# Table cosines by a quarter turn, LayerNorm statistics moved to ScalarE, and a later long-lag tail in an S4 block with a gated MLP

## The chip, the cores and the metric

The kernel runs on one core of a Trainium2 chip. A time is the device time of one execution in microseconds (us), quoted as the median of several executions. Where two kernels are compared, the ratio is the mean time of one kernel's fast runs over that of the other's fast runs of the same rounds, so it is not quite the ratio of the medians. A "span" is the profiled execution alone and is about 2 us shorter than the timed figure.

Five engines work side by side: PE (TensorE, matrix products), DVE (VectorE), ACT (ScalarE), POOL (GpSimd) and SP (which issues the transfers). Each has its own instruction list, and waits tie the lists together. A scheduler orders each list from the program text, so editing one part can reorder others.

## The reference, cut to what matters

```python
h  = x + S4(layernorm(x))               # x is [1, 2048, 640]
h2 = h + MLP(layernorm(h))
# S4: a convolution of length 2048 per channel, with
P = exp(dt*A * l)                       # complex, l = 0..2047, 128 states, 640 channels
K = einsum("dn,dnl,dn->dl", C, P, dt*B).real
y = irfft(rfft(u, 4096) * rfft(K, 4096))[:2048] + u * Dskip
# MLP
out = (sigmoid(x @ w_gate) * (x @ w_up)) @ w_down      # F = 1728
```

The powers `P` are complex exponentials, so building them needs a sine and a cosine of large phases. The kernel builds them from two tables, A and B, in four chunks of 160 channels. It multiplies the tables on PE to get the convolution kernel, and does the convolution with Fourier matrices on PE over four sequence blocks.

## The kernel before

The cosine needed two steps on ScalarE: an absolute value of the phase, in place, and a Sin with a bias from a [128,1] tile of pi/2.

```python
def cos_of(out, ph, scale):
    nc.scalar.activation(ph, ph, AF.Abs)
    act_fn(out, ph, AF.Sin, scale=-scale, bias=hpi[:, 0:1])

def trig_a(c):                                   # sines and cosines of table A, chunk c
    ...
    for k0, n in ((0, 6), (6, 5), (11, 5)):
        ph = tabp.tile([P, 6, W], F32, name="a_ph", tag="ph", bufs=2)
        for k in range(n):
            nc.vector.tensor_scalar(ph[:, k], phi[:, o:o + W], ..., MAGIC16, ALU.mult, ALU.add)
        p16 = ...                                # the low 16 bits of ph, as int16
        act_fn(f(sn), p16, AF.Sin, scale=SIN_SCALE16)
        cos_of(f(cs), p16, SIN_SCALE16)
```

The phase is an fp32 number to which a large constant was added, so its low 16 bits hold the phase modulo one turn. `table_a(c)` multiplies exponentials with these sines and cosines on VectorE; its tile `tabA` has one buffer that every chunk uses in turn. `kmm(c)` multiplies table A by table B on PE into `pk`, ScalarE evicts `pk` to `kts`, and from it come `kv` and `klast`. `forward(b)` is the Fourier transform of sequence block b, with ScalarE evicting `ps_z` to `zs`.

```python
def ln_stats(st, mv, src, r):                    # one row of LN statistics on VectorE
    for hh in range(2):
        nc.vector.bn_stats(st[:, r, hh, :], src(r)[:, 320 * hh:320 * hh + 320])
    nc.vector.bn_aggr(mv[:, r, :], ...)

def ln_stats_act(src, mv, rr, junk):             # the same on ScalarE, two passes a row
    for i, r in enumerate(rr):
        nc.scalar.activation(junk(i), src(i), AF.Identity, accum_out=acc[:, 0, r:r + 1])
    ...
    for i, r in enumerate(rr):
        nc.scalar.activation(junk(i), src(i), AF.Square, bias=acc[:, 0, r:r + 1], accum_out=acc[:, 1, r:r + 1])

    # main order, cut
    for r in range(8):
        ln_stats(st, mv, ur, r)                  # blocks 1 and 2 on VectorE
    ln_stats_act(..., range(8, 16), ...)         # blocks 3 and 4 on ScalarE
    trig_a(0); chain_b(0); norm(0); table_a(0); ...; forward(0); kvs = [kmm(0)]
    trig_a(1); norm(1); chain_b(1); norm(2); norm(3)
    for b in range(1, NB):
        ... forward(b)
    for c in range(NC - 1):
        ...                                      # kmm(c), inverse of c-1, chain_b(c+1)
        Vt = kspec(c, ...)                       # spectra of the kernel, products, long-lag spectra
        table_a(c + 1, ...); trig_b(c + 2); ...; trig_a(c + 2)
    kvs.append(kmm(NC - 1)); ...
    Vl = kspec(NC - 1, ...)                      # its long-lag spectra before the last inverse
    inv0(NC - 1, Vl, ...)
    mlp(...)
```

## Time and profile before

| | before |
|---|---|
| median of 3 runs | 391.68 us (391.44 to 392.13) |
| profiled span | 389.7 us |
| the MLP alone, first Sigmoid (182.4) to the end | 207.3 us |
| second chunk's `kv` complete | 131.9 us |
| the four tables A complete | 54.7, 82.0, 114.0, 156.4 us |

First the profile page of the kernel before: busy time per engine, then the busy share in 40 equal slices of 9.7 us, in tenths. PEclk is PE's granted clock, in tenths of full speed.

```profile
PE 317.8 (82%) x2466; PEld 197.3 (51%) x2466; DVE 290.6 (75%) x659; ACT 266.7 (68%) x481; POOL 13.5 (3%) x16
...
PE   1533378881569899948999999997999999999996
...
DVE  2999998979799869499999899999999222112131
ACT  6988979969969877655556675556765558755500
...
PEclk9976589997769999996999999998999999999999
```

From the 19th slice on, PE is nearly full: that is the MLP. Ahead of it (0 to 180 us) VectorE and ScalarE are the fuller ones in most slices up to the 13th. So a gain has to come from there.

Next the busy time of each engine in three stretches of before. The columns are the stretch, its length, then busy us with instruction counts for PE, PEld, DVE, ACT and POOL, then the granted clock, the DMA share and GB/s.

```profile
96.00:112.00 16.00, 6.79 (x51) 4.47 (x51) 14.04 (x32) 15.99 (x23) 0.00 (x0) 0.71 0.06 22
134.00:157.00 23.00, 21.34 (x357) 19.18 (x355) 18.52 (x42) 18.08 (x35) 0.00 (x0) 1.00 0.28 73
180.00:380.00 200.00, 196.87 (x1118) 104.25 (x1117) 137.35 (x269) 117.90 (x220) 3.70 (x3) 0.99 0.16 56
```

From 96 to 112 ScalarE is busy every moment and PE works 6.8 of 16 us. The timeline of that stretch (start, duration, engine, line, operation) shows why, and what follows from it 35 us later:

```profile
102.76 0.68 ACT L390 CAST zs<-ps_z 128x640 bf16<-128x640 f32 x1
103.33 0.97 ACT L224 ACTIVATE a_cs<-a_ph,hpi 128x800 bf16<-128x800 int16 x1
104.19 0.87 ACT L224 ACTIVATE a_sn<-a_ph 128x800 bf16<-128x800 int16 x1
...
105.34 1.12 ACT L246 ACTIVATE a_ph<-a_ph 128x800 int16<-128x800 int16 x1
...
110.09 0.72 ACT L390 CAST zs<-ps_z 128x640 bf16<-128x640 f32 x1
110.86 3.36 PE L389 MATMUL ps_z<-u,c_G 128*128 128x320 bf16 x12 [4.81 <-ACT zs L390]
...
143.79 0.83 DVE L288 TENSOR_TENSOR tabA<-tabEA,tabE 128x1280 bf16<-128x1280 bf16 x1 [3.49 <-PE pk L409]
```

Two evictions of `ps_z` lie 7.3 us apart, with Sin, Abs, Sin and others between them. PE waits 4.81 us for the second. PE then does what is left of the second chunk (its `kv`) and the third chunk's products late, and VectorE waits 3.49 us for the latter before it may overwrite the table's buffer.

The costliest table-A groups on ScalarE (busy us, mean ns), and one kind of LN pass:

```profile
L246 ACT ACTIVATE a_ph<-a_ph 128x800 int16<-128x800 int16 x8 | 8.9, 1108 | 0.0
L224 ACT ACTIVATE a_cs<-a_ph,hpi 128x800 bf16<-128x800 int16 x8 | 7.8, 970 | 0.0
L224 ACT ACTIVATE a_sn<-a_ph 128x800 bf16<-128x800 int16 x8 | 6.9, 868 | 0.0
L361 ACT ACTIVATE ln_junk<-u,ln_acc 128x640 bf16<-128x640 bf16 x8 | 6.5, 818 | 0.0
L246 ACT ACTIVATE a_ph<-a_ph 128x960 int16<-128x960 int16 x4 | 5.2, 1290 | 0.0
```

### The profile page before, as it was taken

The numbers are of one execution on the slowest core, as the hardware profiler recorded it, in microseconds if no ns is written. First come the engines' busy times: TensorE is split into PE (matmuls) and PEld (weight loads), VectorE is DVE, ScalarE is ACT, GpSimd is POOL, SyncE is SP. The second block draws the span as 40 slices with busy tenths as digits, with TensorE's granted clock in tenths as the row PEclk, the third lists the DMA queues.
The fourth block names the chain that finished last, engine by engine and source line by source line (L and its number), as shares of the span: only waits on it lengthen the run. The fifth ranks groups of instructions, "written<-read, shape, count | busy, mean of one in ns | idle before, by whom it ended". The sixth has DMA issues, their size and how long they took to land.

```text
span 389.7 us, 6462 instructions
## 1 busy us (share of the span) xinstructions
PE 317.8 (82%) x2466; PEld 197.3 (51%) x2466; DVE 290.6 (75%) x659; ACT 266.7 (68%) x481; POOL 13.5 (3%) x16
## 2 busy tenths in 40 slices
PE   1533378881569899948999999997999999999996
PEld 0522156560337788834444664443664445744463
DVE  2999998979799869499999899999999222112131
ACT  6988979969969877655556675556765558755500
POOL 0030200020000000010000100000100000000000
PEclk9976589997769999996999999998999999999999
DMA  7940000431011532699960003000003000010001
GB/s 174 395 199 1 2 0 2 143 149 67 35 67 41 133 103 67 212 276 349 363 238 0 2 2 135 0 3 1 0 17 119 2 0 2 0 69 1 0 19 50
DMA packets 28496, 33.49 MB, mean 86 GB/s; under 512 B 16305, under 2 KB 23858, under 8 KB 28210
## 3 DMA queue, kind: packets, MB, share of 16 engines
q1 hardware_dynamic: 28466, 33.08, 25.5%
q8 instruction: 19, 0.31, 0.3%
q14 instruction: 11, 0.09, 0.1%
HBM read 23.88 MB, written 9.18 MB: 85 GB/s over the span
## 4 chain that ended last, share of the span: by engine, by line
PE 40%; DVE 34%; ACT 17%; DMA 4%; issue 2%; POOL 2%; SPq 1%; DVEq 0%; ACTq 0%; POOLq 0%
PE ml_po L760 11%; PE ml_pu L730 8%; PE ml_pg L730 7%; DVE u L621 5%; DVE u L620 4%; DVE u L624 3%; DVE u L623 3%; ACT zs L390 2%; ACT a_ph L246 2%; ACT a_cs L224 2%; PE ps_xk L461 2%; DVE ml_hm L741 2%; PE ps_z L389 2%; PE pk L409 2%; ACT xk L463 2%
## 5 line engine op out<-in xcount | busy, mean ns | idle before, releaser
L389 PE MATMUL ps_z<-u,c_G 128*128 128x320 bf16 x256 | 46.5, 338 | 29.2 <-ACT Z L390 12.9
L730 PE MATMUL ml_pg<-lnT,Wg 128*128 128x512 bf16 x260 | 66.5, 381 | 0.0
L730 PE MATMUL ml_pu<-lnT,Wu 128*128 128x512 bf16 x260 | 65.7, 383 | 0.0
L760 PE MATMUL ml_po<-Wd,ml_hm 128*128 128x320 bf16 x416 | 61.1, 304 | 0.0
L760 PEld LDWEIGHTS <-ml_hm 128*128 128x128 bf16 x416 | 40.7, 99 | 18.5 <-issue 1.5
L389 PEld LDWEIGHTS <-c_G 128*128 128x128 bf16 x256 | 27.1, 109 | 44.4 <-issue 31.9
L738 ACT ACTIVATE ml_sg<-ml_pg 128x512 bf16<-128x512 f32 x52 | 31.0, 596 | 25.7 <-PE ml_pg L730 19.5
L741 DVE TENSOR_TENSOR ml_hm<-ml_ub,ml_sg 128x512 bf16<-128x512 bf16 x52 | 21.8, 420 | 34.4 <-ACT ml_ub L740 34.4
L740 ACT CAST ml_ub<-ml_pu 128x512 bf16<-128x512 f32 x52 | 30.4, 584 | 22.5 <-PE ml_pu L730 22.4
L730 PEld LDWEIGHTS <-Wu 128*128 128x128 bf16 x260 | 25.6, 99 | 30.8 <-issue 0.5
L730 PEld LDWEIGHTS <-Wg 128*128 128x128 bf16 x260 | 25.6, 99 | 28.1 <-issue 0.6
L620 DVE TENSOR_TENSOR u<-Z,S 128x1280 bf16<-128x1280 bf16 x36 | 29.3, 815 | 0.0
L621 DVE TENSOR_TENSOR u<-Z,S 128x1280 bf16<-128x1280 bf16 x36 | 29.3, 816 | 0.0
L409 PE MATMUL pk<-tabB,tabA 128*128 128x84 bf16 x320 | 17.6, 213 | 12.1 <-ACT kts L410 9.9
L461 PE MATMUL ps_xk<-kv,c_KM 128*128 128x160 bf16 x320 | 24.3, 232 | 2.3 <-ACT xk L463 1.0
L461 PEld LDWEIGHTS <-c_KM 128*128 128x128 bf16 x320 | 22.6, 98 | 3.8 <-issue 3.2
L409 PEld LDWEIGHTS <-tabA 128*128 128x128 bf16 x320 | 15.7, 105 | 15.4 <-issue 11.4
L636 PE MATMUL ps_y<-VR,c_IV 128*128 128x320 bf16 x96 | 19.7, 300 | 2.3 <-ACT ml_ub L740 2.3
L390 ACT CAST zs<-ps_z 128x640 bf16<-128x640 f32 x24 | 15.8, 688 | 7.1 <-DMA dz<-zs 3.8
L624 DVE TENSOR_TENSOR u<-u,u 128x1280 bf16<-128x1280 bf16 x24 | 19.6, 816 | 0.0
L623 DVE TENSOR_TENSOR u<-u,u 128x1280 bf16<-128x1280 bf16 x24 | 19.6, 815 | 0.0
L702 ACT ACTIVATE ln<-h,ln_nmr,ln_rstd 128x640 bf16<-128x640 bf16 x14 | 11.8, 910 | 7.8 <-DVE ln_nmr L369 7.8
(133 smaller groups left out, 518.8 us busy)
## 6 DMA issues: line engine op xcount, KB each, us to landing
dz<-zs SPq DMA_DIRECT2D x12, 320.0 KB, 2.2
Z<-dz SPq DMA_DIRECT2D x6, 640.0 KB, 6.6
u<-in_A_u_dram SPq DMA_DIRECT2D x4, 640.0 KB, 5.8
c_KM<-s4c_KM SPq DMA_DIRECT2D x1, 2560.0 KB, 12.6
h<-in_A_u_dram SPq DMA_DIRECT2D x4, 640.0 KB, 3.8
dxk<-xk SPq DMA_DIRECT2D x16, 160.0 KB, 2.4
S<-dxk SPq DMA_DIRECT2D x4, 640.0 KB, 11.2
Wg<-in_B_w_gate_dram SPq DMA_DIRECT2D x4, 520.0 KB, 6.8
```

What stands on the lines that cost most here:

```text
L389: MM(ps[:, ri, 0:UH], lhsT=G[:, ft, hf, ri, r, :], rhs=us[b][:, r, o:o + UH], start=(r == 0), stop=(r == 3))
L409: MM(pk[:, i, :], lhsT=A[:, ri, g].rearrange("p e c -> p (e c)"), rhs=B[:, ri, :, 4 * g:4 * g + 4], start=(ri == 0), stop=(ri == 1))
L461: MM(ps[:, hf, ri * W:ri * W + W], lhsT=KM[:, ft, hf, ri, KI[d] + q, :], rhs=kv[:, j, :], start=(q == 0), stop=(q == len(KD[d]) - 1))
L620: V(t1[:, 0], z, k[:, :, :, o:o + UH], ALU.mult)
L621: V(t2[:, 0], z, k[:, :, ::-1, o:o + UH], ALU.mult)
L623: V(s1[:], s1[:], t1[:], ALU.add)
L624: V(s2[:], s2[:], t2[:], ALU.add)
L730: nc.tensor.matmul(ps[:], lhsT=W[:, dc, f0:f0 + 128], rhs=lnT[:, dc].rearrange("p a b -> p (a b)"), start=(dc == 0), stop=(dc == 4))
L738: nc.scalar.activation(sg[:], pg[:], AF.Sigmoid)
L740: nc.scalar.copy(ub[:], pu[:])
L741: nc.vector.tensor_tensor(hm[:, ft, :], ub[:], sg[:], ALU.mult)
L760: nc.tensor.matmul(po[k][:, c, 0:320], lhsT=hm[:, ft, 128 * lr:128 * lr + 128], rhs=Wd[:, ft, 320 * c:320 * c + 320], start=(start and ft ...
```

## The change

A quarter turn (0.25 in units of a turn) is added to the fp32 phase on VectorE, after the sine has been taken; the cosine is then a plain Sin with no Abs and no bias tile. In addition:

- LN statistics of block 2 (four rows) go from VectorE to ScalarE, so that blocks 2 to 4 are all done there; their small coefficient steps go to GpSimd.
- The norm of a block stands directly before its forward transform, and block 4 comes later, after `corner(0)`; the scheduler's delays of blocks 3 and 4 (`DELAY`) are lowered.
- In the last chunk the long-lag spectra (`later`) follow the inverse, so that their stores no longer stand ahead of the MLP's weight loads.
- A Sigmoid on a dummy element loads that table early.
- The first input load is split, corner terms are merged into one `edge` tile, and PSUM pools are rearranged.

```diff
         for k0, n in ((0, 6), (6, 5), (11, 5)):
             ...
-            act_fn(f(sn), p16, AF.Sin, scale=SIN_SCALE16)
-            cos_of(f(cs), p16, SIN_SCALE16)
+            act_fn(sn[...], p16(ph, n), AF.Sin, scale=SIN_SCALE16)
+            if phs:
+                cosine(*phs.pop())      # add 0.25 on VectorE, then Sin
+            phs.append((k0, n, ph))
+        cosine(*phs.pop())
...
     def norm(b):
-        ln_coef(mv, rstd, nmr, rs)
+        if b:
+            nc.gpsimd.tensor_scalar(rstd[:, rs], mv[:, rs, 1], 1e-5, None, ALU.add)
+            nc.gpsimd.tensor_tensor(rstd[:, rs], rstd[:, rs], mhalf[:, rs], ALU.pow)
+            nc.gpsimd.tensor_tensor(nmr[:, rs], acc[:, 0, rs], rstd[:, rs], ALU.mult)
+        else:
+            ln_coef(mv, rstd, nmr, rs)
...
-    for r in range(8):
+    for r in range(4):
         ln_stats(st, mv, ur, r)
-    ln_stats_act(lambda i: ur(8 + i), mv, range(8, 16), ...)
     trig_a(0)
+    for b in range(1, NB):
+        ln_stats_act(lambda i: ur(4 * b + i), mv, range(4 * b, 4 * b + 4), ...)
...
-    norm(1)
     chain_b(1)
-    norm(2)
-    norm(3)
-    for b in range(1, NB):
-        forward(b)
+    block(1)                            # norm(b), forward(b), with a lower priority
+    block(2)
...
         corner(c)
+        if c == 0:
+            block(3)
...
+    act_fn(hpi[:], hpi[:], AF.Sigmoid)
     kvs.append(kmm(NC - 1))
...
+    # in the MLP part, after the first LN
+    later()                             # the last chunk's long-lag spectra and their stores
```

More of the change, by code (lines that the diff above doesn't have):

```diff
@@ L28 @@
 LATER2 = 300
-DELAY = (0, 0, 300, 600)
+DELAY = (0, 0, 100, 400)
 B_VAL = [0, 4, 2, 6, 1, 5, 3, 7, 256, 260, 258, 262, 512, 516, 768, 772, 1024, 1280, 1536, 1792, 2048]
@@ L33 @@
 NL = 14
-EDGE = [(0, 0), (0, 1), (0, 2), (0, 3)] + [(b, r) for b in range(3) for r in range(2)] + [(b, 0) for b in range(4)]
-SEL = {(0, 3): (10,), (1, 2): (4,), (1, 3): (11, 4, 5), (2, 2): (6,), (2, 3): (12, 6, 7),
-       (3, 0): (0,), (3, 1): (0, 1), (3, 2): (8, 0, 1, 2), (3, 3): (13, 8, 9, 0, 1, 2, 3)}
+EDGE = [(b, 0) for b in range(4)] + [(b, r) for b in range(3) for r in range(2)] + [(0, r) for r in range(4)]
+SEL = {(0, 3): (0,), (1, 2): (4,), (1, 3): (1, 4, 5), (2, 2): (6,), (2, 3): (2, 6, 7),
+       (3, 0): (10,), (3, 1): (10, 11), (3, 2): (8, 10, 11, 12), (3, 3): (3, 8, 9, 10, 11, 12, 13)}
 SELI = {k: i for i, k in enumerate(SEL)}
@@ L81, in host_consts @@
         sel[list(rows), i, 31] = 1.0
+    sel[32, SELI[0, 3], 31] = 1.0
     pick = np.zeros((P, 4, 32))
@@ L91, in host_consts @@
     one = np.zeros((P, 32))
-    one[0, 0] = 1.0
+    one[64, 0] = 1.0
     return {"ident": np.eye(P), "G": G.reshape(P, -1), "KM": KM.reshape(P, -1), "IV": IV.reshape(P, -1), "sel": sel.reshape(P, -1),
@@ L143, in full_kernel @@
     ktp = sc.pool("kts", bufs=2)
-    psk = sc.pool("ps_k", bufs=2, space=PSUM)
+    psk = sc.pool("ps_k", bufs=2, space=PSUM, side="right")
     ps2 = sc.pool("ps_2", bufs=3, space=PSUM)
@@ L159, in full_kernel, with load_u @@
     dl = cp.tile([P, 2, 5], BF16, name="dl")
-    def load_u(b):
-        sy.dma_start(us[b][:], xh[b])
+    def load_u(b, n=4):
+        for r in range(0, 4, n):
+            sy.dma_start(us[b][:, r:r + n], xh[b, :, r:r + n])
     sy.dma_start(dl[:, 0], ins["A_log_dt"].rearrange("(c p) -> p c", p=P))
@@ L169, in full_kernel @@
         if k == 0:
-            load_u(0)
+            load_u(0, 1)
     for b in range(1, NB):
@@ L178, in full_kernel @@
     sel = cload(cp, "sel", [P, len(SEL), 32])
-    dsk = cp.tile([1, D], BF16, name="dsk")
-    sy.dma_start(dsk[:], ins["A_Dskip"].rearrange("(o d) -> o d", o=1))
+    edge = cp.tile([96, D], BF16, name="edge")
+    sy.dma_start(edge[64:65, :], ins["A_Dskip"].rearrange("(o d) -> o d", o=1))
     uh = cp.tile([NL, D], BF16, name="uhead")
@@ L269, in trig_a, with cosine @@
         sn = tabp.tile([P, W // 4, 16, 4], BF16, name="a_sn")
+        phs = []
+        p16 = lambda ph, n: ph[:, 0:n].bitcast(I16).rearrange("p k (g c t) -> p k g c t", c=4, t=2)[:, :, :, :, 0]
+        def cosine(k0, n, ph):
+            nc.vector.tensor_scalar(ph[:, 0:n], ph[:, 0:n], 0.25, None, ALU.add)
+            act_fn(cs[:, :, k0:k0 + n, :].rearrange("p g k c -> p k g c"), p16(ph, n), AF.Sin, scale=SIN_SCALE16)
         for k0, n in ((0, 6), (6, 5), (11, 5)):
@@ L273, in trig_a @@
                 nc.vector.tensor_scalar(ph[:, k], phi[:, o:o + W], 4.0 * (31 - 2 * (k0 + k)) * 2.0 ** -32, MAGIC16, ALU.mult, ALU.add)
-            p16 = ph[:, 0:n].bitcast(I16).rearrange("p k (g c t) -> p k g c t", c=4, t=2)[:, :, :, :, 0]
-            f = lambda t: t[:, :, k0:k0 + n, :].rearrange("p g k c -> p k g c")
-            act_fn(f(sn), p16, AF.Sin, scale=SIN_SCALE16)
-            cos_of(f(cs), p16, SIN_SCALE16)
+            act_fn(sn[:, :, k0:k0 + n, :].rearrange("p g k c -> p k g c"), p16(ph, n), AF.Sin, scale=SIN_SCALE16)
+            if phs:
+                cosine(*phs.pop())
+            phs.append((k0, n, ph))
+        cosine(*phs.pop())
         T["tr", c] = cs, sn
@@ L399, in kmm @@
         kv = ktp.tile([P, 5, W], BF16, name="kv")
-        kr = ktp.tile([NL, W], BF16, name="klast", bufs=1)
         A, B = T["A", c], T["B", c]
@@ L408, in product, with diagonal @@
                     for ri in range(2):
-                        MM(pk[:, i, :], lhsT=A[:, ri, g].rearrange("p e c -> p (e c)"), rhs=B[:, ri, :, 4 * g:4 * g + 4], start=(ri == 0), stop=(ri == 1))
+                        last_mm[0] = MM(pk[:, i, :], lhsT=A[:, ri, g].rearrange("p e c -> p (e c)"), rhs=B[:, ri, :, 4 * g:4 * g + 4], start=(ri == 0), stop=(ri == 1)).ins
                 nc.scalar.copy(kts[:, g0:g0 + GS, :], pk[:])
-        def diagonal(g1, kts):
+        def diagonal(g1, kts, mm):
             ps = ps2.tile([P, 2, 512], F32, name="ps_kv", tag="p2")
@@ L417, in diagonal @@
             dc = slice(o + 4 * g1, o + 4 * g1 + 4 * GC)
-            MM(ps[0:32, 0, 0:4 * GC], lhsT=one[0:1, :], rhs=dsk[0:1, dc], start=True, stop=False, tile_position=(0, 0))
+            with tc.issue_after(mm):
+                MM(ps[0:32, 0, 0:4 * GC], lhsT=one[64:65, :], rhs=edge[64:65, dc], start=True, stop=False, tile_position=(64, 0))
             for c4 in range(4):
@@ L425, in diagonal @@
             for c4 in range(4):
-                for i, q in enumerate((80, 64, 48)):
+                for i, q in enumerate((48, 64, 80)):
                     MM(pl[:, :, c4], lhsT=last[:, i, c4, :], rhs=kts[:, :, q + c4], start=(i == 0), stop=(i == 2))
             nc.scalar.copy(kv[:, :, 4 * g1:4 * g1 + 4 * GC], ps[:, 0, 0:20 * GC].rearrange("p (j x) -> p j x", j=5))
-            nc.scalar.copy(kr[:, 4 * g1:4 * g1 + 4 * GC], ps[0:NL, 1, 0:4 * GC])
-        prev = None
+            nc.scalar.copy(edge[0:NL, dc], ps[0:NL, 1, 0:4 * GC])
+        prev, last_mm = None, [None]
         for g1 in range(0, G4, GC):
@@ L436, in kmm @@
                 diagonal(*prev)
-            prev = (g1, kts)
+            prev = (g1, kts, last_mm[0])
         diagonal(*prev)
-        return kv, kr
+        return kv
     def fold_back(Vt, t1, t2, fs, w):
@@ L460, in spec @@
                     for q, j in enumerate(KD[d]):
-                        MM(ps[:, hf, ri * W:ri * W + W], lhsT=KM[:, ft, hf, ri, KI[d] + q, :], rhs=kv[:, j, :], start=(q == 0), stop=(q == len(KD[d]) - 1))
+                        mm = MM(ps[:, hf, ri * W:ri * W + W], lhsT=KM[:, ft, hf, ri, KI[d] + q, :], rhs=kv[:, j, :], start=(q == 0), stop=(q == len(KD[d]) - 1)).ins
+            if d == 0:
+                T["mm"] = mm
             dst = S01[:, d, ft, :, :, o:o + W] if d < 2 else xks[:, d - 2, ft]
@@ L480, in kspec, with later @@
             prod((0, 1))
-        for d in range(1, NB):
-            for ft in range(2):
-                spec(d, ft)
-        for d in range(2):
-            for ft in range(2):
-                sy.dma_start(dxk[d, :, ft, :, :, o:o + W], xks[:, d, ft])
-        return Vt
+        def later():
+            for d in range(1, NB):
+                for ft in range(2):
+                    spec(d, ft)
+            for d in range(2):
+                for ft in range(2):
+                    sy.dma_start(dxk[d, :, ft, :, :, o:o + W], xks[:, d, ft])
+        return Vt, later
     def inv0(c, Vt, fs=((0, 1),), done=None):
@@ L495, in inv0 @@
         for a in range(2):
-            MM(pv[:, a], lhsT=ident[:], rhs=hv[:, a], start=True, stop=False)
+            with tc.issue_after(T["mm"]):
+                MM(pv[:, a], lhsT=ident[:], rhs=hv[:, a], start=True, stop=False)
             if a:
-                MM(ps[96:128, a, W:2 * W], lhsT=sel[0:NL, SELI[0, 3], :], rhs=kl[:, o:o + W], start=False, stop=False, tile_position=(0, 96))
+                MM(ps[96:128, a, W:2 * W], lhsT=sel[32:33, SELI[0, 3], :], rhs=edge[32:33, o:o + W], start=False, stop=False, tile_position=(32, 96))
         for fg in fs:
@@ L515, in full_kernel @@
     bases_b(0)
-    for r in range(8):
+    for r in range(4):
         ln_stats(st, mv, ur, r)
-    ln_stats_act(lambda i: ur(8 + i), mv, range(8, 16), lambda i: prp.tile([P, D], BF16, name="ln_junk", tag="y")[:])
     trig_a(0)
+    for b in range(1, NB):
+        ln_stats_act(lambda i: ur(4 * b + i), mv, range(4 * b, 4 * b + 4), lambda i: prp.tile([P, D], BF16, name="ln_junk", tag="y")[:])
     chain_b(0)
@@ L529, in full_kernel, with block @@
     kvs = [kmm(0)]
-    trig_a(1)
-    norm(1)
-    chain_b(1)
-    norm(2)
-    norm(3)
-    for b in range(1, NB):
+    def block(b):
         tc.cur_priority += DELAY[b]
+        norm(b)
         forward(b)
         tc.cur_priority -= DELAY[b]
+    trig_a(1)
+    chain_b(1)
+    block(1)
+    block(2)
     IV = cload(yp, "IV", [P, 4, 2, 2, P], tag="u1")
@@ L548, in full_kernel @@
     h = hs[0]
-    kl = uh
     def corner(c):
         cs = slice(W * c, W * c + W)
-        V(kl[:, cs], kvs[c][1][:], uh[:, cs], ALU.mult)
+        V(edge[32:33, cs], edge[0:1, cs], uh[0:1, cs], ALU.mult)
     for c in range(NC - 1):
@@ L559, in full_kernel @@
         corner(c)
-        Vt = kspec(c, kvs[c][0], prp, yp)
+        if c == 0:
+            block(3)
+        Vt, later = kspec(c, kvs[c], prp, yp)
+        later()
         table_a(c + 1, 2 if c == NC - 2 else 1)
@@ L576, in full_kernel @@
     corner(NC - 1)
-    Vl = kspec(NC - 1, kvs[NC - 1][0], prp, yp)
+    Vl, later = kspec(NC - 1, kvs[NC - 1], prp, yp)
     for r in range(4):
@@ L586, in full_kernel @@
     inv0(NC - 1, Vl, fs=((0,), (1,)), done=done)
-    sc.close("ps_2", "ps_k", "kts")
+    sc.close("ps_k", "kts")
     ZR = [Z0]
@@ L604, in full_kernel, with edges, far @@
     gu = load_gu(nc, wp, ins)
-    load_h(1)
     Wd = load_d(nc, xp, ins)
-    for b in (2, 3):
-        load_z(b)
-        load_s(b)
     VR = {}
+    def edges():
+        V(uh[:], edge[0:NL], uh[:], ALU.mult)
+    def far():
+        later()
+        for b in (2, 3):
+            load_z(b)
+            load_s(b)
     def products(b):
@@ L637, in inverse @@
                     if (b, s) in SELI and not ft:
-                        MM(ps[96:128, 0:UH], lhsT=sel[0:NL, SELI[b, s], :], rhs=kl[:, o:o + UH], start=False, stop=False, tile_position=(0, 96))
+                        MM(ps[96:128, 0:UH], lhsT=sel[0:NL, SELI[b, s], :], rhs=uh[:, o:o + UH], start=False, stop=False, tile_position=(0, 96))
                 hv = hs[b][:, s, o:o + UH]
@@ L643, in inverse @@
                 yield
-    mlp(tc, sc, xp, yp, cp, hs, st2, gu, Wd, ident, oh, ln_coef, ln_stats_act, products, inverse, load_h)
+    mlp(tc, sc, xp, yp, cp, hs, st2, gu, Wd, ident, oh, ln_coef, ln_stats_act, far, edges, products, inverse, load_h)
     sc.close("stream", "weights", "yp", "prod", "xp", "consts", "dram")
@@ L673, in load_d, with mlp @@
     return Wd
-def mlp(tc, sc, xp, yp, cp, hs, st, gu, Wd, ident, oh, ln_coef, ln_stats_act, products, inverse, load_h):
+def mlp(tc, sc, xp, yp, cp, hs, st, gu, Wd, ident, oh, ln_coef, ln_stats_act, later, edges, products, inverse, load_h):
     nc = tc.nc
@@ L680, in mlp @@
     tmp = sc.pool("ml_tmp", bufs=2)
-    psg_p = sc.pool("ml_psg", bufs=2, space=PSUM)
-    psu_p = sc.pool("ml_psu", bufs=2, space=PSUM)
-    pso_p = sc.pool("ml_pso", bufs=2, space=PSUM)
+    psg_p = sc.pool("ml_psg", bufs=2, space=PSUM, side="right")
     mv = big.tile([P, 16, 2], F32, name="ln2_mv")
@@ L691, in prep @@
         r0 = 4 * b
-        ln2 = lns[b] = yp.tile([P, 4, 640], BF16, name="ln2", tag="u0")
+        ln2 = lns[b] = yp.tile([P, 4, 640], BF16, name="ln2", tag="u0" if b else "u3")
         if b:
@@ L718, in mlp @@
     prep(0)
+    tc.cur_priority += LATER
+    later()
+    tc.cur_priority -= LATER
     turn(0)
+    load_h(1)
+    sc.close("ps_2")
+    psu_p = sc.pool("ml_psu", bufs=2, space=PSUM)
+    pso_p = sc.pool("ml_pso", bufs=2, space=PSUM)
     tc.cur_priority += LATER
+    edges()
     products(1)
```

## The prediction

> What bounds it now. One core; the profiled span is 389.7 us, the median 391.68. From about 178.5 us on it is the MLP: by the busy time per stretch, PE is busy 203 of the 210 us from 180 to 390, at a clock near 1, and its longest wait there is 2.3 us. So the MLP takes about 211 us whatever precedes it; a gain must come from the 178 us ahead.
>
> There the bound alternates. From 10 to 54.6 us VectorE is busy 90 to 100% (timeline); the first tabA ends at 54.6 and releases PE. From 63 to 82 and 88 to 140 the chain of waits runs through ScalarE's Sin, Abs, Sin of table A and the zs evictions, while VectorE is 92% busy; it waits about 11 us in all from 82 to 157. From 157 to 178 it is a relay of PE, ScalarE and VectorE for the last chunk.
>
> Removed, added, moved.
> - Twelve Abs on a_ph (8 of 1.108 us, 4 of 1.290) leave ScalarE: about 13 us. The cosines lose their bias tensor: 970 against 868 ns for one shape with and without it, 1.2 us in all. The Trainium skill, "ScalarE: Activation LUTs", "What ACT_TABLE_LOAD costs", gives about 93 ns per pointer operand; the trace shows 102.
> - Twelve fp32 adds come to VectorE. A 640-wide fp32 one in SBUF took 0.475 us; "VectorE: DVE Perf Modes", "The perf-mode tier table", puts it in the 2x mode. Estimate from it: 0.64 and 0.56 us, 7 us in all. VectorE was nearly the bottleneck, so this eats half of the gain.
> - LN statistics of four rows leave VectorE (0.86 us a row, 3.4 us, in the first 22 us) and cost ScalarE 1.53 us a row, 6 us, mostly later; small coefficient steps go to GpSimd.
> - Scheduled order: norms of blocks 2 to 4 follow the first tabA; block 4's forward transform comes later; the first chunk's products precede chain_b of the last.
> - Last chunk: two of four xk evictions with their spectra follow the inverse, and dxk writes no longer block weight loads (queue held from 162 to 170). About 1.2 us.
> - The early Sigmoid load takes 1.28 us off ScalarE at 179.4, but the ml_pg it serves ended later: no gain.
>
> Sum along the new order. First tabA ends near 48 instead of 54.6, but chain_b now ends after it, near 50: kmm starts 4 to 5 us earlier. ScalarE, with the LN rows, reaches the first kts only near 57, so most of this is lost; second tabA ends 1 us earlier (82.0 before), the third about 1.5, with the first products done. From there to the last tabA (156.4) VectorE waits less: 5 to 7 us earlier. MLP starts 6 to 8.5 us earlier; I allow some for new waits.
>
> Predicted 384.5 us, range 380.5 to 389. Faster by over 2%: 0.42; within 2%: 0.57; slower: 0.01.
>
> What would show it: first kmm product at 49 to 51 us; no a_ph Abs; new adds of 0.55 to 0.65 us; ScalarE busy about 9 us less; VectorE about 3 us more, with less idle between 82 and 157; last tabA end 149 to 152; first ml_pu near 171; from there to the end 210 to 212 us.
>
> What would make it wrong: ScalarE's extra LN rows delaying Z, kts and zs evictions more than I sum; zs waiting for its DMA as before (3.0 us at 81); slower adds; VectorE waits in the new order; or, for more gain, the MLP shortening with earlier weights.

## The result, and the profile after

The changed kernel took 385.28 us (385.07 to 385.80, 4 runs) against 391.85 (391.44 to 392.13, 4 runs). The ratio of the fast runs is 0.9835, with a 95% interval of 0.9818 to 0.9852. That is 1.65% faster, within 2%, and 0.8 us above the prediction. The profiled span is 383.1 us.

The page after, and the same stretches:

```profile
PE 315.6 (82%) x2451; PEld 199.7 (52%) x2466; DVE 292.7 (76%) x660; ACT 260.4 (68%) x486; POOL 22.6 (6%) x22
...
PEclk9995667998699789978999999998999999999999
```

```profile
96.00:112.00 16.00, 13.18 (x133) 10.08 (x133) 15.96 (x35) 15.88 (x27) 0.00 (x0) 0.79 0.16 62
134.00:157.00 23.00, 20.52 (x353) 18.05 (x353) 16.91 (x37) 13.44 (x29) 0.00 (x0) 0.94 0.22 56
180.00:380.00 200.00, 195.70 (x1118) 105.00 (x1130) 134.81 (x264) 114.41 (x214) 3.37 (x3) 0.99 0.14 51
```

ScalarE is as full from 96 to 112 as before (15.88 of 16 us), but PE now works 13.2 us instead of 6.8: what the Abs held is spent on evictions. In the timeline they come without the gap, and VectorE waits for PE at the table 0.36 us and not 3.49:

```profile
103.22 0.71 ACT L405 CAST zs<-ps_z 128x640 bf16<-128x640 f32 x1
103.80 0.95 ACT L424 CAST kts<-pk 128x420 bf16<-128x420 f32 x2
104.60 1.33 ACT L405 CAST zs<-ps_z 128x640 bf16<-128x640 f32 x2
...
135.91 0.82 DVE L298 TENSOR_TENSOR tabA<-tabEA,tabE 128x1280 bf16<-128x1280 bf16 x1 [0.36 <-PE pk L423]
```

The groups that answer to those of before (from the lists of ScalarE and of VectorE):

```profile
L371 ACT ACTIVATE ln_junk<-u,ln_acc 128x640 bf16<-128x640 bf16 x12 | 9.8, 822 | 0.0
L226 ACT ACTIVATE a_cs<-a_ph 128x800 bf16<-128x800 int16 x8 | 6.8, 872 | 0.0
L371 ACT ACTIVATION_READ_ACCUMULATOR ln_junk<-u,ln_acc 128x1 f32 x12 | 2.3, 193 | 0.0
...
L276 DVE TENSOR_SCALAR a_ph<-a_ph 128x800 f32<-128x800 f32 x8 | 4.6, 569 | 0.0
L276 DVE TENSOR_SCALAR a_ph<-a_ph 128x960 f32<-128x960 f32 x4 | 2.6, 652 | 0.1
```

Where the 6.6 us of span came from, in us from the start, by the timelines:

| point | before | after | after earlier by |
|---|---|---|---|
| first table A complete | 54.7 | 47.0 | 7.7 |
| first `kts` | 55.9 | 55.6 | 0.3 |
| second table complete | 82.0 | 79.9 | 2.1 |
| third table complete | 114.0 | 112.8 | 1.2 |
| second chunk's `kv` complete | 131.9 | 119.1 | 12.8 |
| fourth table complete | 156.4 | 151.3 | 5.1 |
| last product V | 168.0 | 162.9 | 5.1 |
| MLP's first transpose | 175.9 | 169.9 | 6.0 |
| first Sigmoid | 182.4 | 175.8 | 6.6 |
| from there to the end | 207.3 | 207.3 | 0 |

The early lead of 7.7 us shrinks to 1.2. The gain is made again between the third and the fourth table (42.4 us before, 38.5 after), in the stage in which VectorE had waited for PE. The last 1.5 us come between V and the first Sigmoid.

### The profile page after: what moved, and what is told of

The parts are those of the page before. It is cut to its first block, busy times and chain, and to the rows that moved or that the text cites. A ratio compares the mean times of both kernels' runs of the same rounds, so it can differ in the third digit from the quotient of the medians.

```text
span 383.1 us, 6461 instructions
## 1 busy us (share of the span) xinstructions
PE 315.6 (82%) x2451; PEld 199.7 (52%) x2466; DVE 292.7 (76%) x660; ACT 260.4 (68%) x486; POOL 22.6 (6%) x22
## 4 chain that ended last, share of the span: by engine, by line
PE 42%; DVE 29%; ACT 18%; DMA 4%; issue 3%; SPq 1%; POOL 1%; ACTq 0%; POOLq 0%; DVEq 0%
PE ml_po L799 11%; PE ml_pu L769 8%; PE ml_pg L769 8%; DVE u L653 4%; DVE u L654 4%; DVE u L657 3%; PE pk L423 3%; DVE u L656 2%; PE ps_z L404 2%; ACT ln_junk L371 2%; ACT zs L405 2%; DVE ml_hm L780 2%; DMA Wg<-in_B_w_gate_dram 2%; PE ps_xk L476 2%; ACT ln_junk L368 2%
## 5 line engine op out<-in xcount | busy, mean ns | idle before, releaser
L769 PE MATMUL ml_pg<-lnT,Wg 128*128 128x512 bf16 x250 | 65.2, 380 | 0.4
L769 PE MATMUL ml_pu<-lnT,Wu 128*128 128x512 bf16 x255 | 64.8, 380 | 0.4 <-issue 0.2
L404 PE MATMUL ps_z<-u,c_G 128*128 128x320 bf16 x256 | 41.3, 320 | 22.1 <-ACT Z L405 19.6
L404 PEld LDWEIGHTS <-c_G 128*128 128x128 bf16 x256 | 26.1, 103 | 34.5 <-issue 23.4
L423 PE MATMUL pk<-tabB,tabA 128*128 128x84 bf16 x320 | 20.7, 236 | 19.0 <-ACT kts L424 17.4
L423 PEld LDWEIGHTS <-tabA 128*128 128x128 bf16 x320 | 18.8, 121 | 21.5 <-issue 19.0
L378 POOL TENSOR_TENSOR ln_rstd<-ln_rstd,mhalf 128x4 f32<-128x4 f32 x4 | 4.8, 1197 | 238.5 <-DVE ln_rstd L377 238.5
```

Source lines behind the costliest of these rows:

```text
L404: MM(ps[:, ri, 0:UH], lhsT=G[:, ft, hf, ri, r, :], rhs=us[b][:, r, o:o + UH], start=(r == 0), stop=(r == 3))
L423: last_mm[0] = MM(pk[:, i, :], lhsT=A[:, ri, g].rearrange("p e c -> p (e c)"), rhs=B[:, ri, :, 4 * g:4 * g + 4], start=(ri == 0), stop=(ri ...
L769: nc.tensor.matmul(ps[:], lhsT=W[:, dc, f0:f0 + 128], rhs=lnT[:, dc].rearrange("p a b -> p (a b)"), start=(dc == 0), stop=(dc == 4))
```

## The experiments

Twelve kernels ran, in three calls of four. The kernels ran beside runs of the kernel before. Its medians were 391.28, 391.22 and 393.13 us (11 runs each). For the first four I held one theory, T1: the table-A cosine is the main gain. The rival, T2, was that the new order and the LN move carry it, and that the cosine matters little.

### e1_abs_back: the changed kernel with the old cosine

```diff
...
-            if phs:
-                cosine(*phs.pop())
-            phs.append((k0, n, ph))
-        cosine(*phs.pop())
...
+            cos_of(f(cs), p16, SIN_SCALE16)      # Abs, then Sin with bias
```

> The changed kernel with the Abs put back for table A's cosines (twelve Abs on ScalarE, bias tensor, no adds on VectorE); all else as changed. Theory 1 (the gain is ScalarE's relief from the Abs, and shows between 88 and 136 us): 4 to 6 us slower than the changed kernel, 389 to 391. Theory 2 (the gain is the new order and the LN rows leaving VectorE; the Abs were only traded for adds on a full VectorE): at most 1.5 us slower, 385.5 to 387.

Measured: 394.14 us (393.01 to 396.54), ratio to before 1.0070 (1.0040 to 1.0101). That is about 9 us slower than the changed kernel and slower than before. Both theories missed: the cosine matters more than T1 had it, inside this kernel. Its stretch, and its waits of VectorE between 82 and 158 us (total, times, longest):

```profile
96.00:112.00 16.00, 7.90 (x71) 5.95 (x71) 11.57 (x29) 15.70 (x23) 0.00 (x0) 0.50 0.06 22
```

```profile
DVE tabA L290 <- PE pk L415: 6.2, 2, 3.7
DVE tabMB L266 <- ACT tabMB L226: 5.6, 3, 5.0
```

PE is back at 7.9 of 16 us and VectorE waits 6.2 us for it. In the same window before had 4.3 us of this wait and the changed kernel 0.4:

```profile
DVE edge L576 <- ACT edge L444: 4.4, 1, 4.4
...
DVE tabA L298 <- PE pk L423: 0.4, 1, 0.4
```

(The wait of 4.4 us for `edge` shown for the changed kernel stands after its last table, at 152 to 156.6.)

### e2_cos_alone: the kernel before with the new cosine only

> The kernel before with only the new cosine of table A (no Abs, no bias, one fp32 add each on VectorE). Theory 1: 3 to 5 us faster than before, 387 to 389. Theory 2: within 1 us of before, since VectorE is about full there and gets 7 us more.

The edit is the first hunk of the diff above, put into the kernel before. Measured: 389.15 us (388.89 to 392.03), ratio 0.9961 (0.9926 to 0.9996). That is a gain of 2.1 us by the medians (1.5 by the ratio, 0.2 to 2.9 by its interval), less than the 3 to 5 of T1. PE works 12.8 of the 16 us from 96 to 112, and the second chunk's `kv` is complete at 118.1 instead of 131.9. The mechanism is there with the cosine alone, but less of it reaches the end: in its profile the first Sigmoid comes 3.5 us earlier (178.9), and from there to the end it takes 1.2 us longer (208.5).

### e3_ln_dve: the changed kernel with block 2's LN statistics on VectorE

```diff
-    for r in range(4):
+    for r in range(8):
         ln_stats(st, mv, ur, r)
-    for b in range(1, NB):
+    for b in range(2, NB):
         ln_stats_act(...)
```

> The changed kernel with the LN statistics of block 2 put back on VectorE, eight rows there as before (and its coefficients as before). Theory 1: within 1 us of the changed kernel, 384.3 to 386.3, because the first kts eviction was no earlier than before (55.7 against 55.9 us) although the first tabA ended 7.7 us earlier. Theory 2: 3 us or more slower, 388 or more.

Measured: 388.59 us (387.80 to 390.19), ratio 0.9931 (0.9904 to 0.9958), 3.3 us slower than the changed kernel. T1 misses and T2's number fits, but not for the reason I had in mind: its tables are not late: the fourth ends at 151.7 (151.3 in the changed kernel). The loss lies after it, in the last chunk, which I had not thought of. e9 takes that up.

### e4_spectra_early: the changed kernel with the long-lag spectra in their old place

```diff
     Vl, later = kspec(NC - 1, kvs[NC - 1], prp, yp)
+    later()
...
-        later()
```

> The changed kernel with the last chunk's long-lag spectra in their old place, ahead of the inverse. As predicted: 1 to 1.6 us slower than the changed kernel, 386 to 387. If blocked weight loads counted: 3 us or more slower. If the order does not matter because PE and ScalarE had the time anyway: within 0.4 us.

Measured: 386.05 us (385.00 to 386.66), ratio 0.9855 (0.9828 to 0.9881): 0.8 us slower by the medians, with intervals that overlap. The stores stand ahead of the weight loads again. A gap opens in the transfer queue between a weight load that ends its issue at 157.2 and the stores that begin at 162.37; the changed kernel issues weights all through it. Yet the first transpose comes only 0.4 us later (170.3 against 169.9). The prediction's 1.2 us is not contradicted and not settled.

### e8_abs_ln: both large parts undone

> The changed kernel with both large parts undone: the Abs cosine is back, and the LN statistics of the second block are back on VectorE. Undone one at a time they cost about 9 us (394.1) and 3.3 us (388.6). Theory A, the parts add up: 397 to 398 us. Theory B, the LN rows on ScalarE only pay where the Abs have left: with Abs in place they are better on VectorE, so this one is faster than the kernel with Abs back alone, 388.5 to 391.5 us, and its second to fourth tables end earlier than in that one.

The edits of e1 and e3 together. Measured: 393.01 us (390.53 to 394.41), ratio 1.0036 (1.0003 to 1.0068). Theory A (the parts add up to 397 or 398) falls. Theory B has the right sign, since e8 is 1.1 us faster than e1, and its second to fourth tables do end 0.6 to 1.0 us earlier, but it expected more than that, and the two intervals overlap. With e1, e3 and the changed kernel this makes a two-by-two table (us, ratio to before), all in the new order:

| | LN of block 2 on VectorE | on ScalarE | |
|---|---|---|---|
| old cosine (Abs) | e8: 393.01, 1.0036 | e1: 394.14, 1.0070 | LN move +1.1 |
| new cosine (add) | e3: 388.59, 0.9931 | changed: 385.28, 0.9835 | LN move -3.3 |
| | cosine -4.4 | cosine -8.9 | |

The rest of the change, without the cosine and the LN move, is no gain at all: e8 is slower than before by 0.4%. And the LN move shows a gain only where the Abs have gone.

### e9_ln_dve_filled: e3 with PE kept busy in one gap

PE in e3 stands idle for 4.17 us before the last chunk's products, and after that its products are slow. Here 20 products into an unused PSUM tile fill the gap; the result is untouched.

```diff
+        if c in (3,):
+            pw = psk.tile([P, GS, 84], F32, name="pk", tag="k")
+            with tc.issue_after(T["spec"]):      # after the spectra of the chunk before
+                for _ in range(20):
+                    MM(pw, lhsT=ident, rhs=<420 columns of chunk 3's sines>, start=True, stop=True)
```

> The kernel with the LN rows of the second block back on VectorE (388.6 us, 3.3 slower than the changed one), plus 20 products of no use, 128x420 each, that PE runs in its idle gap of 4.2 us before the last chunk's products (result untouched). Theory C, the loss came from the granted clock: after that gap PE ran at half clock from 147.5 to 156.8 in the last chunk, where the changed kernel ran at full clock; filled, the clock stays at 1.00 there, a product of 128x84 takes 47 ns and not 79, and 2 to 3 us come back: 385.6 to 386.8 us. Theory D, the loss is the 3.4 us of statistics on VectorE: it stays at 388 to 389.5.

The timeline of PE around the gap, first in e3, then in e9:

```profile
147.66 3.09 PE L423 MATMUL pk<-tabB,tabA 128*128 128x84 bf16 x40 [4.17 <-DVE tabA L303]
...
151.90 1.58 PE L423 MATMUL pk<-tabB,tabA 128*128 128x84 bf16 x20
```

```profile
145.21 3.71 PE L450 MATMUL pk<-a_sn,c_ident 128*128 128x420 bf16 x20
...
149.55 0.92 PE L423 MATMUL pk<-tabB,tabA 128*128 128x84 bf16 x20 [0.62 <-DVE tabA L303]
...
153.64 0.93 PE L423 MATMUL pk<-tabB,tabA 128*128 128x84 bf16 x20
```

Twenty products take 1.58 us in e3 and 0.93 in e9. The stretches of e3 by the microsecond show the granted clock (third number from the end) drop while PE is idle, and stay low for some 10 us:

```profile
145.00:146.00 1.00, 0.00 (x0) 0.00 (x0) 1.00 (x2) 0.00 (x0) 0.00 (x0) 1.00 1.11 273
146.00:147.00 1.00, 0.00 (x0) 0.00 (x0) 1.00 (x3) 0.00 (x0) 0.00 (x0) 0.83 0.45 111
147.00:148.00 1.00, 0.34 (x6) 0.34 (x7) 1.00 (x2) 0.00 (x0) 0.00 (x0) 0.50 0.00 0
...
156.00:157.00 1.00, 1.00 (x13) 0.33 (x11) 0.00 (x0) 0.62 (x3) 0.00 (x0) 0.55 0.95 113
```

The Trainium skill, "TensorE: Matmul & The Clock Gate", "Part 1: The HAM clock gate", says that PE's clock falls to half after an idle window of about 3.4 us and comes back after a busy one of that length, and that this window runs freely and isn't reset by the kernel. The clock records of all 14 traces agree with the windows: the switches of a trace lie whole steps of 3.41 us apart (in e3 those at 126.17, 133.00, 146.65, 156.89 and 170.55 are 2, 4, 3 and 4 steps apart). So the time to a switch depends on where a gap lies. In e3 PE stopped at 143.5 and the clock fell at 146.65; before the MLP it fell 5.0 us after PE stopped in the kernel before, and 2.1 in the changed one. But a window need not be idle throughout. Take e5 and then e2: PE has a gap of 1.95 us in each, from 143.08 in e5 and from 147.79 in e2. The stretches are cut at the clock's own steps:

```profile
142.24:145.65 3.41, 1.47 (x27) 1.14 (x25) 3.41 (x7) 2.14 (x4) 0.00 (x0) 1.00 0.67 164
145.65:149.06 3.41, 2.86 (x49) 2.54 (x47) 3.41 (x7) 2.00 (x4) 0.00 (x0) 0.50 0.12 28
```

```profile
145.39:148.80 3.41, 2.00 (x20) 1.36 (x19) 3.41 (x7) 1.23 (x2) 0.00 (x0) 1.00 0.69 168
148.80:152.21 3.41, 1.87 (x40) 1.72 (x41) 3.41 (x6) 1.61 (x4) 0.00 (x0) 1.00 0.00 0
```

In e5 the gap lies in one window, PE is busy for 43% of it, and the clock falls at its end. In e2 the same gap is split between two windows, with 59 and 55%, and the clock stays. Counted over the 14 traces (from 20 us on), 84 of 85 windows at full clock with PE busy under 45% ended in a fall, 4 of 17 with 45 to 54%, and none of 1145 above that. At half clock, none of 111 windows with PE busy under 70% ended in a return, 21 of 37 with 70 to 88%, and all 68 above that. In e3 the window in which the products began again and the next one were 71 and 88% busy, and only the third, full one brought the clock back at 156.9, over 9 us after that beginning.

From the fourth table to the last V, e3 takes 14.0 us, e9 11.5, and the changed kernel 11.6. So the half clock cost the last chunk 2.5 us in that profile, and filling the gap took it back.

The total says less: e9 measured 387.96 us (387.38 to 388.25), ratio 0.9907 (0.9885 to 0.9928), only 0.6 us faster than e3, where theory C expected 2 to 3. In e9's profile the second table is already 1.5 us later than in e3's, and the fourth 1.9, although the instructions up to there are the same. The clock had dropped around 58 us in e9's execution (0.50 from 58 to 60), and not in e3's. So what a single profile shows of the clock in the first 60 us varies between executions. Another 1.1 us went at the MLP's entry, where e9 takes 7.1 us from the first transpose to the first Sigmoid and e3 6.0: the clock came back 7.6 us after that transpose in e9 and 4.7 in e3. Theory C is shown for the last chunk. That it makes up the whole 3.3 us of the LN move is not shown.

### e10_filled_mlp: the changed kernel with PE kept busy before the MLP

```diff
+    pw = psg_p.tile([P, 512], F32, name="ml_pg", tag="ml_pg")
+    for _ in range(18):
+        nc.tensor.matmul(pw[:], lhsT=ident[:], rhs=hs[0][:, 3, 128:640], start=True, stop=True)
     turn(0)
```

> The changed kernel, plus 18 products of no use, 128x512 each, on PE in its idle gap of 4.4 us before the MLP's first transposes. Theory C, the clock: in the changed kernel PE ran at 0.50 from 168 to 174.5 us, with the MLP bound by PE; filled, it runs at 1.00 there and the kernel is 2 to 3 us faster, 382.3 to 383.5 us. Rival: the MLP's entry is set by the LN coefficients, the evictions of the transposes and the weights' DMA; then within 0.8 us of the changed kernel's 385.3.

Measured: 384.08 us (383.91 to 384.98), ratio 0.9815 (0.9791 to 0.9838), 1.2 us less than the changed kernel (the intervals of the two ratios overlap). It was run at another time. In its profile the first transpose comes at 169.8, as without the fill, and the first Sigmoid 4.9 us later; in two profiles of the changed kernel it was 5.9 and 7.1. The size falls between the two theories: PE is at full clock there, and then waits up to 1.04 us at a time for the evictions of the transposes.

### e5_no_sigmoid: the changed kernel without the early Sigmoid

```diff
-    act_fn(hpi[:], hpi[:], AF.Sigmoid)
```

> The changed kernel without the early Sigmoid. The prediction said that the early table load brings nothing, as the first gate product ended later than the load: then 384.7 to 385.9 us, the load of 1.28 us standing before the first Sigmoid with ScalarE waiting for PE after it. If the early load counts: 386.4 to 386.8 us.

Measured: 384.82 us (383.56 to 385.64), ratio 0.9831 (0.9806 to 0.9856), the same as the changed kernel. The early load brings nothing, as predicted. It isn't without effect: in both kernels without it (e5, e11) PE's gap before the last chunk's products is 1.95 us and not 1.47, the clock falls there for one window of 3.4 us, and from the fourth table to V they take 12.1 us (11.6 with the load), after tables that ended earlier (149.1 and 149.9).

### e12_after_again: the changed kernel once more

> The changed kernel once more, as a control beside the others of this call. 384.9 to 385.8 us, its four tables of A ending within 0.5 us of the first profile's 47.0, 79.9, 112.8 and 151.3, PE at full clock from 140 to 164 and at half clock where the MLP begins. If the clock drops at different places in a second profile of the same code, then what the profile showed of it is chance of that execution, and single profiles can't carry the theory.

Measured: 384.96 us (384.06 to 385.93), ratio 0.9802 (0.9769 to 0.9835; the runs of before beside it were slower). The tables end at 47.6, 80.2, 112.0 and 150.5, which is 0.35 to 0.85 us from the first profile and so a little wider than I expected. PE was at full clock from 140 to 164 in both, and at half clock where the MLP begins, for 6.8 us in the first profile and 10.2 in this one; so the time from the first transpose to the first Sigmoid was 5.9 us and then 7.1. The stages up to V repeat; differences of 1 us between two profiles mean nothing here, nor those of 1.2 at the MLP's entry.

### e7_no_add: the changed kernel without the add

```diff
-            nc.vector.tensor_scalar(ph[:, 0:n], ph[:, 0:n], 0.25, None, ALU.add)
```

> The changed kernel without the quarter-turn add: table A's cosines come out as sines, the result is wrong on purpose. It takes 12 adds, about 7.3 us, off VectorE. If VectorE bounds the table stages, as the prediction had it when it said that the adds eat half of the gain: 380.5 to 383 us. If ScalarE bounds them: 384.3 to 386. The scheduler orders anew, which may shift either by 1 us.

Measured: 383.43 us (382.22 to 383.99), ratio 0.9753 (0.9720 to 0.9787); the result is wrong (relative error 0.064). That is 1.5 us faster than the changed kernel (384.96). The 7.2 us of adds cost 1.5 us of time. The expectation for a VectorE bound (380.5 to 383) missed by 0.4, and that for ScalarE alone (384.3 to 386) by 0.9: neither engine is the bound alone. Between 82 and 158 us VectorE waits 5.7 us for `edge` and 4.9 for `tabMB`, both from ScalarE, more than with the adds (4.4 and 4.3).

### e6_block4_early: the changed kernel with block 4 in its old place

```diff
-DELAY = (0, 0, 100, 400)
+DELAY = (0, 0, 300, 600)
     block(2)
+    block(3)
...
-        if c == 0:
-            block(3)
```

> The changed kernel with norm and forward transform of the fourth block back in their old place, before the first products. Theory B (ScalarE is what is short in the first 110 us): its evictions and LN work stand before the second table, 386.5 to 389 us. If the place of block 4 doesn't matter: 384.6 to 386.

Measured: 389.17 us (387.92 to 390.75), ratio 0.9909 (0.9877 to 0.9942), 4.2 us slower than the changed kernel. The size is the expected one, the reason is not: the third table is even earlier (110.7). The fourth is late (153.2), PE idles 4.58 us before it, and then runs at half clock from 148 to 158. From the fourth table to V it takes 14.1 us, as in e3. In its profile the late table (1.8 us) and this stage (2.5) make up nearly all of the loss.

### e11_filled_no_sigmoid: e5 and e10 together

> The changed kernel without the early Sigmoid and with the 18 products of no use that keep PE busy before the MLP (384.08 us with the fill alone, 384.82 without the Sigmoid alone). If both add up: 383.2 to 384.2 us, faster than the changed kernel and so the best of all. If the Sigmoid's table load now stands on the way, as the gate product ends earlier: 384.6 to 385.8.

Measured: 384.33 us (383.31 to 385.59), ratio 0.9793 (0.9756 to 0.9829). It is 0.6 us below the changed kernel. The gain of the fill shows in the stage (4.9 us from the first transpose to the first Sigmoid), but in the total it is within what two sets of runs of one kernel differ by. e10 and e11 beat the kernel before; that either beats the changed kernel is not shown.

### The stages side by side

All from the timelines; us.

| kernel | second `kv` complete | PE busy, 96 to 112 | fourth table complete | fourth table to V | first transpose to first Sigmoid |
|---|---|---|---|---|---|
| before | 131.9 | 6.8 | 156.4 | 11.6 | 6.5 |
| e1 (Abs back) | 127.9 | 7.9 | 157.5 | 13.8 | 6.9 |
| e8 (Abs and LN back) | 126.9 | 8.9 | 156.5 | 13.8 | 6.9 |
| e2 (cosine alone) | 118.1 | 12.8 | 153.8 | 10.8 | 6.0 |
| e3 (LN back) | 116.0 | 14.4 | 151.7 | 14.0 | 6.0 |
| e6 (block 4 early) | 120.6 | 12.9 | 153.2 | 14.1 | 6.1 |
| changed | 119.1 | 13.2 | 151.3 | 11.6 | 5.9 |
| changed again (e12) | 118.3 | 13.7 | 150.5 | 11.6 | 7.1 |

Two things sort the kernels. Those with the Abs have PE idle from 96 to 112 and the second `kv` after 126. Those in which PE went to half clock in the last chunk (e1, e8, e3, e6) take 13.8 to 14.1 us from the fourth table to V, the others 10.8 to 11.6. The last column differs as much between the two profiles of the changed kernel as between kernels.

## Why the prediction was right or wrong

The total was right: 384.5 predicted, 385.28 measured, inside 380.5 to 389, and in the class held likeliest (within 2%). The single steps:

- *The MLP takes about 211 us whatever precedes it.* Right: 210.2 us from the first up product (172.9) to the end, 211.2 before, and 207.3 from the first Sigmoid in both kernels.
- *First table near 48, first product 49 to 51, first `kts` near 57, second table 1 us earlier, third 1.5.* Right or near: 47.0, 49.9, 55.6, 2.1 and 1.2. Most of the first lead is lost again, as the sum had it.
- *Last table at 149 to 152, MLP 6 to 8.5 us earlier, first up product near 171.* Right for the table: 151.3. The MLP came at the low edge: 6.0 us earlier by the first transpose, 6.6 by the first Sigmoid, but 5.6 by the prediction's own mark, the first up product (172.9, after 178.5).
- *VectorE waits less between 82 and the last table.* Right. Its waits from 82 to 158 us summed to 11.2 us before, and to 10.9 after, of which 4.4 for `edge` follow the last table. The wait for PE fell from 4.3 to 0.4.
- *The adds take 0.64 and 0.56 us.* Right: 0.65 and 0.57. The step that failed stands next to it: "VectorE was nearly the bottleneck, so this eats half of the gain." Removing the 7.2 us of adds bought 1.5 us (e7). The adds mostly fill time in which VectorE would have waited for ScalarE or PE.
- *ScalarE busy about 9 us less, VectorE about 3 more.* 6.3 less and 2.1 more. Neighbouring instructions of ScalarE overlap by about 0.1 us in the trace; with overlaps counted once, the Abs gave back 12.8 us (about 13 predicted), the bias 0.8 (1.2), and the LN rows cost 6.1 (6). These terms fit. What the prediction had no term for is that the evictions of `zs`, `kts` and `S` took 1.5 us more; that is not traced further.
- *The early Sigmoid: no gain.* Right (e5, 384.82 against 385.28).
- *Late spectra, 1.2 us.* 0.8 by the medians (e4), not settled.
- *What the sum hid.* The prediction added the parts. They don't add: the cosine is worth 2.1 us in the kernel before, 4.4 in the new order with the old LN, and 8.9 with the new one. It traced the whole new order rather than pricing each part, and its stage times held. That the total came within 0.8 us is in part luck: it charged the adds too much, credited ScalarE with too much, and knew nothing of the clock, and these errors don't all point the same way. Nothing in its terms says that the rest alone loses, as e8 does.
- *What it never mentioned.* The clock of PE. In e1, e3, e6 and e8 PE fell to half clock in the last chunk, and each took 2.2 to 2.5 us more there than the changed kernel, which kept a gap of only 1.47 us before it. Part of what the LN move and block 4's place are worth is this, by the profiles; e9 took it back in the stage and only 0.6 us of it in the total. What makes up the rest of the LN move's 3.3 us stays open.

That the Abs are what keeps PE idle there is shown by the sorting above: in seven kernels, with the Abs PE works 6.8 to 8.9 us of those 16, and without them 12.8 to 14.4, whatever else differs. The same sorting holds for VectorE's wait for PE's products before a table, from 82 to 158 us: 4.3, 6.2 and 6.2 us with the Abs, at most 0.4 without. That ScalarE's queue is the link is read from the waits. That this alone makes the 3.9 us between the third and the fourth table is argued from the waits, not isolated, as the scheduler reorders other work with it.

## What to carry to other kernels

Cost an engine's saving by what its freed time releases: here 13 us off ScalarE mattered because evictions stand in the same queue as the Sins, and PE and then VectorE waited for them. Parts of a tuned change can be worth nothing, or less, without each other, so undo each alone and two together before saying which one paid. And when an edit makes PE's earlier work end sooner but not what it waits for, look at the granted clock after the gap: a longer gap can cost more than the time that was won (e6: third table 2.1 us earlier, last chunk 2.5 us longer).

## What the Trainium skill lacked or had wrong

- "TensorE: Matmul & The Clock Gate", "HAM oscillation": its rule is that PE should have no idle gaps over about 3.4 us. Shorter ones were enough here. In e1 the clock fell at 157.39 though PE's longest gap in the window before was 1.02 us (PE was busy 52% of it), and came back at 160.81. (The page's next section, "A second HAM failure mode", tells of a clock that swings through short idling, without a figure.) How busy a window has to be, the page doesn't say. By the count under e9 the clock fell after windows under about half busy, stayed at half up to 70%, and always came back above 88%; between, both happened.
- The same page, "Part 1": it puts back-to-back products at N / 2.4 GHz + 2.5 ns warm and N / 1.2 GHz cold, which is 37.5 and 70 ns for N = 84. With a new stationary operand for each product, 20 of them took 0.93 us (47 ns each) at full clock and 1.58 us (79 ns) at half. For such pairs the page has about 81 ns at N = 128 ("Back-to-back issue gap"), and no figure for a smaller N or for half clock.
- "ScalarE: Activation LUTs", "What ACT_TABLE_LOAD costs": 1283 ns for the load agrees with the trace (1.28). The drain of 1380 ns that it adds isn't seen here. In the changed kernel the instruction before a load ended at 94.12, the load ran from 94.15 to 95.43, and the next Sin began at 95.44.

```profile
93.67 0.45 ACT L226 ACTIVATE tabE<-lre 128x320 bf16<-128x320 f32 x1
94.15 1.28 ACT L226 ACT_TABLE_LOAD   x1
95.44 1.76 ACT L226 ACTIVATE a_sn<-a_ph 128x960 bf16<-128x960 int16 x2
```

- The same page gives the cost of an ACTIVATE, but none for the accumulator output: each pass with one is followed by a read that is recorded with 0.19 us. It overlaps the pass before it and the next one, so it adds less: in the changed kernel passes began at 43.25 and 43.97 us, with the read at 43.88.
- "GPSIMD Engine Reference", "Specifications", says that GpSimd shares its SBUF interfaces with VectorE, and with which VectorE instructions it clashes, but not what this costs a tiny operation. ("SBUF — State Buffer", "Who interferes with whom", says that whichever comes second is blocked for the other's whole instruction; the longest VectorE instruction beside these steps took 1.48 us.) The same 128x4 step took 2.90 and 3.29 us in two cases and 0.35 in a third. No run isolates the cause, and spans on GpSimd are rough:

```profile
36.72 2.90 POOL L384 TENSOR_SCALAR rstd<-mv 128x4 f32<-128x4 f32 x1 [18.85 <-DVE mv L373]
...
43.84 3.29 POOL L384 TENSOR_SCALAR rstd<-mv 128x4 f32<-128x4 f32 x1
...
51.65 0.35 POOL L384 TENSOR_SCALAR rstd<-mv 128x4 f32<-128x4 f32 x1 [2.81 <-DVE mv L373]
```
